# Two start-up loads of a fused attention and feed-forward kernel: issued by ScalarE instead of SyncE

## The chip, the cores and the metric

The kernel runs on one core of a Trainium2 chip. The metric is the device time of one execution in microseconds (us); lower is better. The engines are TensorE (PE; its weight loads are PEld), VectorE (DVE), ScalarE (ACT), GpSimd (POOL) and SyncE (SP). SyncE does no arithmetic: it issues data transfers (DMA), which 16 DMA engines carry out.

## The reference, cut to what matters

```python
def _attn_ref(q, k, v):                      # 8 batches, 8 heads, 576 tokens, head size 64
    scores = (1 / np.sqrt(D)) * np.matmul(q, k.transpose(0, 1, 3, 2))
    rel = pos[:, None] - pos[None, :]
    mask_local   = (rel >= 0) & (rel < 32)
    mask_strided = (rel >= 0) & (pos[None, :] % 32 == pos[:, None] % 32)
    # heads 0 to 3 use mask_local, heads 4 to 7 mask_strided
    scores = np.where(masks[None], scores, -1e9)
    ...                                      # softmax over the keys
    return np.matmul(attn, v)

def _moe_ref(x, w_in, w_out):                # 4608 tokens, 512 -> 2048 -> 512
    h = x @ w_in
    g = 0.5 * h * (1.0 + erf(h * inv_sqrt2))
    return g @ w_out
```

The attention's output, heads side by side, is the input x of the feed-forward part.

## The kernel before, in words

The 4608 tokens are worked on in nine tiles of 512. For each tile the feed-forward part runs over 16 slices of 128 hidden units. For each slice, `ffn_h` makes the hidden values H (lines L758 to L760), `ffn_g` applies the activation, and `ffn_o` adds the slice's share of the output O (L796 to L798). Each product is done three times with operands split into a high and a low part, to keep fp32 precision. The weights of a slice come as `ws` and are split on ScalarE and VectorE (`split_w`, L174 to L189). This product work keeps TensorE busy, and the attention of the later tiles is fitted in beside it on the other engines.

The first tile's attention has nothing to hide behind. It is done on TensorE, in the order that the string `START` writes out, one item after the other:

- **Local heads.** `local_job` (items L0 to L3) does four local tiles of 128 tokens. Item by item: scores S_L (L322), mask and maximum on VectorE (L280, four each), exponentials on ScalarE (L285, four each), sums and reciprocals on VectorE (L289, L292), the scaling (L298 on VectorE for tiles 2, 0 and 3, L301 on ScalarE for tile 1), transposes (L328), a copy (L330), values (L336), and the split into high and low parts (L305, L307). The order is tile 2, then 0, 1 and 3.
- **Strided heads.** `half_tile` (items a0, b0) does the two halves, called A0 and A1 here: scores (L455), mask added on VectorE with `smask` (L464), maximum (L466), difference (L468), exponential on ScalarE (L470), sum (L472), reciprocal and scaling (L474 to L478), transposes (L482) and a copy (L484). `strided_tile` (item A0 of the string) then multiplies by the values (L498), turns the result (L503) and splits it (L506, L509).
- **Fillers.** L949 multiplies zeros into a bank named busy.

The loads: q2, q0, q1 and q3 fetch queries and keys of the local tiles (`load_jq`, L222, tile `qk`, 128 rows of 2,560 B each); S0 and T0 fetch the strided queries and keys of the two halves (`load_half`, L423, tile `qka`, 128 rows of 6,144 B each, 0.786 MB); v1, v0, v2 and v3 the local values (`load_jv`, L229, tile `vl`, rows of 2,048 B); w and W items weights (`load_w`, L153), in two halves for slices 0 and 1; B0 the strided values (`load_b`, L441, tile `va`). "w0" is the weights of slice 0. Before the change all of them are issued by SyncE, in the order of the string. A transfer takes one of eight completion semaphores in turn (DMAHW0 to DMAHW7), and so the ninth waits until the first has landed, and so on.

`behind` attaches a wait from a list `hold` to a transfer; the list is filled by items p alone, which come much later. GpSimd makes the masks: `mask` (L872 to L879) for L280, `ident` (masks.py) for the transposes, `smask` (L883, L884 and L886 on VectorE), and `bmask` (L910 to L918), used first by the second tile. The order on each engine is fixed when the program is built.

Of the kernel before, what the change touches and what calls it, by code (L numbers as in the profile page):

```python
# [86 lines left out]
def attn_ffn_kernel(ctx: ExitStack, tc: tile.TileContext, qk, vl, qka, va, qs, ks, vs, s1, w, out):  # L87
    nc = tc.nc
# [42 lines left out]
    def slot(name, shape, dtype=F32):  # L131

        return wpool.tile(shape, dtype, name=name, tag="w")

    def pace(ins, after):
        if after is not None:
            tc.add_manual_dep(ins.ins, after.ins.name, mybir.DependencyInfo(
                mybir.DependencyClass.Sync, mybir.DependencyReason.DATA), reason="pace")
# [3 lines left out]
    def behind(ins):  # L142

        while hold:
            pace(ins, hold.pop())
        return ins
# [272 lines left out]
    def load_half(o):  # L419

        x = slot(f"qka_{o}", [P, 4 * DM])
        n = N2 * NGR // 2 * 32
        behind(nc.sync.dma_start(x[:, 0:3 * n], qka[0, o]))  # L423
        qa[o] = x
        kv[o] = x[:, 2 * n:3 * n].rearrange("p (a g m) -> p a g m", a=N2, m=MA)
        qv[o] = x[:, 0:2 * n].rearrange("p (n c) -> p n c", c=2 * 32)

    def load_a(t):

        nv = NGR // 4 * HL * D  # L430
        load_half(0)
        vt = slot(f"va_{t}", [P, 4 * DM])
        p = vt[:, nv:nv + NGR * 32].rearrange("p (g m) -> p g m", g=NGR)
        nc.gpsimd.memset(p, 0.0)
        ka[t] = (
                 vt[:, 0:nv].rearrange("p (c h d) -> p c h d", c=NGR // 4, h=HL),
                 p, vt[:, nv + NGR * 32:nv + 2 * NGR * 32].rearrange("p (c q) -> p c q", q=P),
                 qa[0][:, 0:NGR * D].rearrange("p (b c e m) -> p b c e m", b=4, c=NGR // 4, e=DH), vt[:, 0:nv])
# [75 lines left out]
    for vi in range(NA, NV):  # L514
        n = VISITS[vi][2]
# [465 lines left out]
    with tc.manual_schedule(engines={ET.DVE, ET.Activation, ET.PE, ET.SP, ET.Pool}):  # L981
        for it in START:
            kind = it[0]
            if kind == "p":
                hold.append(last[0])
            elif kind in "wWqvSTBEeKkVGg":
                x = int(it[1:] or 0)
                {"w": lambda x: load_w(x, 0 if f"W{x}" in START else None), "W": lambda x: load_w(x, 1),
                 "T": lambda x: load_half(1), "k": lambda x: load_keys_half(x, 1), "q": load_jq, "v": load_jv, "S": load_a, "B": load_b,
                 "E": lambda x: [load_strided(order_g[0], nm) for nm in "qk"],  # L990
                 "e": lambda x: load_strided(order_g[0], "v"),
                 "K": lambda x: load_keys(x, halves=kparts if f"k{x}" in START else None), "V": load_values,
                 "G": lambda x: [load_strided(order_g[1], nm) for nm in "qk"],
                 "g": lambda x: load_strided(order_g[1], "v")}[kind](x)
            else:
                if it not in running:
                    running[it] = job(it)
                if next(running[it], True) is None:
                    continue
                running[it] = None  # L1000
# [218 lines left out]
```

## Time and profile before

| | |
|---|---|
| median of 3 runs | 846.77 us (846.35 to 846.95) |
| profiled execution | 848.29 us |
| its span in the profile | 846.5 us |
| TensorE, busy share of the span | 99% |
| VectorE | 76% |
| ScalarE | 52% |
| GpSimd | 2% |
| mean granted clock of TensorE | 0.996 of full speed |

The span runs from the first to the last instruction of the profiled execution; 1.79 us of its time lie outside. Busy shares are means over a long kernel. The change touches the first 20 us alone, so rows of that stretch are read one by one further down.

### The profile page before, as it was taken

To read this page: it belongs to the slowest core of one execution; us is meant where nothing else is said; L and a number is where in the kernel's file an instruction comes from. 1 tells how busy PE (TensorE), PEld (TensorE's weight loads), DVE (VectorE), ACT (ScalarE), POOL (GpSimd) and SP (SyncE) were. 2 spreads that over 40 slices of the span, in tenths; PEclk is the share of its full clock that TensorE was granted. 3 is DMA by queue.
4 is the path that set the end of the run, shared out by engine and by line. 5 is a ranking of instruction groups with operands and counts; after the bars stand their busy time and mean duration, and the time that the engine had idled before them with its cause. 6 is when DMAs were issued, how large, how long until landed. Compare 5 with 4: busy or idle time off the path is not lost.

```text
span 846.5 us, 15032 instructions
## 1 busy us (share of the span) xinstructions
PE 838.3 (99%) x5442; PEld 690.0 (82%) x5442; DVE 640.3 (76%) x1859; ACT 441.0 (52%) x862; POOL 18.1 (2%) x88
## 2 busy tenths in 40 slices
PE   8999999999999999999999999999999999999997
PEld 5788888888888888888888888888888888888886
DVE  6899989995999589958999698878887988521110
ACT  6898866552664355544553266545552456332222
POOL 5000000000000000000000000000000000000000
PEclk9899999999999999999999999999999999999999
DMA  9965241211220220223021222112102310100001
GB/s 342 416 256 194 64 144 52 68 37 64 99 63 14 92 101 9 69 60 136 7 63 35 78 86 69 42 63 100 60 13 93 101 38 13 36 34 17 1 0 50
DMA packets 27978, 69.40 MB, mean 82 GB/s; under 512 B 5888, under 2 KB 14208, under 8 KB 25856
## 3 DMA queue, kind: packets, MB, share of 16 engines
q1 hardware_dynamic: 27904, 68.44, 22.9%
q8 instruction: 43, 0.70, 0.3%
q14 instruction: 31, 0.25, 0.1%
HBM read 54.78 MB, written 9.44 MB: 76 GB/s over the span
## 4 chain that ended last, share of the span: by engine, by line
PE 98%; POOL 1%; DVE 1%; issue 0%; ACT 0%; POOLq 0%
PE H L758 16%; PE H L759 15%; PE H L760 15%; PE O L796 15%; PE O L798 15%; PE O L797 15%; PE S_x L404 2%; PE S L363 1%; PE S_L L336 0%; PE busy L949 0%; PE A L498 0%; PE S_L L328 0%; POOL bmask L913 0%; PE A L455 0%; POOL bmaskNone L913 0%
## 5 line engine op out<-in xcount | busy, mean ns | idle before, releaser
L798 PE MATMUL O<-w,gl 128*128 128x512 f32 x576 | 224.1, 389 | 0.0
L797 PE MATMUL O<-w,gh 128*128 128x512 f32 x576 | 224.1, 389 | 0.0
L796 PE MATMUL O<-w,gh 128*128 128x512 f32 x576 | 224.1, 389 | 0.0
L766 ACT ACTIVATE H<-H 128x512 f32<-128x512 f32 x144 | 83.8, 582 | 259.7 <-PE H L760 252.1
L770 DVE TENSOR_TENSOR gl<-H,gh 128x512 fp32r<-128x512 f32 x144 | 99.1, 688 | 157.4 <-ACT gh L768 157.3
L768 ACT CAST gh<-H 128x512 fp32r<-128x512 f32 x144 | 84.5, 587 | 118.2 <-PE O L797 113.7
L797 PEld LDWEIGHTS O<-w,gh 128*128 128x128 f32 x576 | 108.2, 188 | 22.6
L798 PEld LDWEIGHTS O<-w,gl 128*128 128x128 f32 x576 | 108.1, 188 | 22.4
L796 PEld LDWEIGHTS O<-w,gh 128*128 128x128 f32 x576 | 108.1, 188 | 22.4
L758 PE MATMUL H<-dh,w 128*128 128x512 f32 x288 | 114.3, 397 | 0.0
L759 PE MATMUL H<-dl,w 128*128 128x512 f32 x288 | 112.3, 390 | 0.0
L760 PE MATMUL H<-dh,w 128*128 128x512 f32 x288 | 112.2, 390 | 0.0
L759 PE MATMUL H<-xl,w 128*128 128x512 f32 x288 | 112.2, 390 | 0.0
L758 PE MATMUL H<-xh,w 128*128 128x512 f32 x288 | 112.2, 389 | 0.0
L760 PE MATMUL H<-xh,w 128*128 128x512 f32 x288 | 112.1, 389 | 0.0
L653 DVE TENSOR_TENSOR av<-sv,sc 128x320 f32<-128x320 f32 (+12 forms) x192 | 102.1, 564 | 6.8 <-DMA sv<-in_vs_dram 6.5
L601 DVE TENSOR_TENSOR qk<-sk,sq 128x320 f32<-128x320 f32 (+5 forms) x200 | 103.6, 545 | 0.0
L605 DVE TENSOR_REDUCE sc<-qk 128x5 f32<-128x320 f32 (+5 forms) x200 | 102.4, 538 | 0.0
L657 DVE TENSOR_REDUCE acc<-av 128x32 f32<-128x544 f32 (+16 forms) x192 | 101.2, 556 | 0.2
L766 ACT ACT_TABLE_LOAD x51 | 65.4, 1283 | 0.9
L758 PEld LDWEIGHTS H<-dh,w 128*128 128x128 f32 x288 | 54.2, 188 | 12.2
L760 PEld LDWEIGHTS H<-dh,w 128*128 128x128 f32 x288 | 54.1, 188 | 11.5
(123 smaller groups left out, 802.8 us busy)
## 6 DMA issues: line engine op xcount, KB each, us to landing
ws<-in_w_dram SPq DMA_DIRECT2D x14, 1023.8 KB, 9.9
qk<-in_qk_dram SPq DMA_DIRECT2D x8, 1280.0 KB, 5.6
vl<-in_vl_dram SPq DMA_DIRECT2D x8, 1024.0 KB, 4.8
out_dram<-ob SPq DMA_DIRECT2D x32, 256.0 KB, 2.3
sk<-in_ks_dram SPq DMA_DIRECT2D x8, 576.0 KB, 4.9
sv<-in_vs_dram SPq DMA_DIRECT2D x8, 576.0 KB, 3.8
band<-PT_L SPq DMA_DIRECT2D x224, 16.0 KB, 1.8
sq<-in_qs_dram SPq DMA_DIRECT2D x4, 448.0 KB, 3.6
```

Source lines behind the costliest of these rows:

```text
L601: nc.vector.tensor_tensor(tmp, sq[vi, "k"][:, c0:c1, :], sq[vi, "q"][:, r0 + r, :].unsqueeze(1).to_broadcast([P, n, D]), ALU.mult)
L605: nc.vector.tensor_reduce(ss[u][:, r, c0:c1], at[0], AX.X, ALU.add)
L653: nc.vector.tensor_tensor(tmp, sq[vi, "v"][:, d0:d1, 0:wr], ss[u][:, r, 0:wr].unsqueeze(1).to_broadcast([P, n, wr]), ALU.mult)
L657: nc.vector.tensor_reduce(ss[u, "acc"][:, r, d0:d1], at[0], AX.X, ALU.add)
L758: last[0] = nc.tensor.matmul(hp, w1[f][:, 0, c, :], xh, start=(i == 0), stop=False)
L759: last[0] = nc.tensor.matmul(hp, w1[f][:, 0, c, :], xl, start=False, stop=False)
L760: last[0] = nc.tensor.matmul(hp, w1[f][:, 1, c, :], xh, start=False, stop=(i == NC - 1))
L766: gelu[n] = nc.scalar.activation(hp, hp, AF.Gelu)
L770: nc.vector.tensor_tensor(gl, hp, gh.bitcast(F32), ALU.subtract)
L796: last[0] = nc.tensor.matmul(o, gh[:, sl], w2[f][:, 0, :], start=(f == 0), stop=False)
L797: last[0] = nc.tensor.matmul(o, gh[:, sl], w2[f][:, 1, :], start=False, stop=False)
L798: last[0] = nc.tensor.matmul(o, gl[:, sl], w2[f][:, 0, :], start=False, stop=(f == NF - 1))
```

## The change

```diff
@@ load_half @@
         x = slot(f"qka_{o}", [P, 4 * DM])
         n = N2 * NGR // 2 * 32
-        behind(nc.sync.dma_start(x[:, 0:3 * n], qka[0, o]))
+        nc.scalar.dma_start(x[:, 0:3 * n], qka[0, o])
         qa[o] = x
```

`load_half` runs twice, for S0 and T0. At both places `hold` is empty, so leaving `behind` out takes no wait away. The transfers now stand in ScalarE's order and use ScalarE's queue. The orders of TensorE and VectorE are the same as before; those of ScalarE, SyncE and GpSimd differ.

On ScalarE, at the start of the program (`early` holds tile 2's scores, `pbig` those of tile 0; a + is a row of the change alone):

```order
 L1215 UNCONDITIONAL_BRANCH
+L423 DMA qka_242<-in_qka_dram 128x1536
 L889 ACT_TABLE_LOAD
 L889 ACTIVATE warm<-warm 128x1
 L285 ACTIVATE early,ss_L_213<-early,nm_L_212 128x96 x4
+L423 DMA qka_254<-in_qka_dram 128x1536
 L285 ACTIVATE pbig,ss_L_227<-pbig,nm_L_226 128x96 x4
```

The first half's transfer (qka_242) became ScalarE's first instruction; the second half's (qka_254) stands behind the four exponentials of local tile 2.

On SyncE, before, with the semaphores that an issue waits for (qk are the local queries and keys, vl the local values, ws_312 the weights of slice 0, ws_375 those of slice 1):

```order
L222 DMA qk_91<-in_qk_dram 128x640 x3
L423 DMA qka_242<-in_qka_dram 128x1536
L423 DMA qka_254<-in_qka_dram 128x1536
L222 DMA qk_91<-in_qk_dram 128x640
L229 DMA vl_276<-in_vl_dram 128x512 x2
L229 DMA vl_276<-in_vl_dram 128x512 [waits DMAHW0_49]
L153 DMA ws_312<-in_w_dram 128x2048 [waits DMAHW1_49]
L441 DMA va_244<-in_va_dram 128x1024 [waits DMAHW2_49]
L153 DMA ws_375<-in_w_dram 128x2048 [waits DMAHW3_49]
L153 DMA ws_312<-in_w_dram 128x2047 [waits DMAHW4_49]
L229 DMA vl_276<-in_vl_dram 128x512 [waits DMAHW5_49]
```

and in the change:

```order
L222 DMA qk_91<-in_qk_dram 128x640 x4
L229 DMA vl_276<-in_vl_dram 128x512 x2
L229 DMA vl_276<-in_vl_dram 128x512 [waits DMAHW0_49]
L153 DMA ws_312<-in_w_dram 128x2048 [waits DMAHW1_49]
L441 DMA va_244<-in_va_dram 128x1024 [waits DMAHW2_49]
L153 DMA ws_375<-in_w_dram 128x2048 [waits DMAHW3_49]
L153 DMA ws_312<-in_w_dram 128x2047 [waits DMAHW4_49]
L229 DMA vl_276<-in_vl_dram 128x512 [waits DMAHW5_49]
```

The two transfers are gone from SyncE. The semaphores went to other transfers, though. Before, numbers 0 to 5 were those of q2, q0, q1, the first and the second strided half, and q3. Now they are those of the first strided half, q2, q0, q1, q3 and the second strided half. So the fourth value transfer, which waited for q3 (DMAHW5), now waits for the second strided half.

On GpSimd, before, around the making of `ident` and `smask` (bmaskNone is one of the masks for the second tile, va the strided probabilities' zero fill):

```order
L878 COPY pbig<-pbig 128x64
L879 MEMSET pbig 128x32
masks.py:197 MEMSET ident 128x128
L434 MEMSET va_244 128x512
L910 MEMSET bmaskNone 128x64
masks.py:199 AFFINE_SELECT ident<-ident 128x128
L883 IOTA smask 32x32 x4
L913 AFFINE_SELECT bmaskNone<-bmaskNone 32x64
L915 AFFINE_SELECT bmaskNone<-bmaskNone 32x64
```

and in the change, the same place and what leads up to it:

```order
L876 AFFINE_SELECT pbig<-pbig 64x96
L915 AFFINE_SELECT bmaskNone<-bmaskNone 32x64
L913 AFFINE_SELECT bmaskNone<-bmaskNone 32x64
L878 COPY pbig<-pbig 128x64
L879 MEMSET pbig 128x32
masks.py:197 MEMSET ident 128x128
L915 AFFINE_SELECT bmaskNone<-bmaskNone 32x64
L913 AFFINE_SELECT bmaskNone<-bmaskNone 32x64
masks.py:199 AFFINE_SELECT ident<-ident 128x128
L883 IOTA smask 32x32 x4
L915 AFFINE_SELECT bmaskNone<-bmaskNone 32x64
```

Seven of the eight L913 and L915 of bmaskNone, which all followed `smask`, now stand ahead of it (four of them are seen here, three further up); the fills of va and bmaskNone moved ahead of `mask`.

## Rows read from the trace of the kernel before

**Rows 1.** The page: busy time, share and instructions of TensorE, and the chain that ended last, its share by engine.

```profile
PE 838.3 (99%) x5442; PEld 690.0 (82%) x5442; DVE 640.3 (76%) x1859; ACT 441.0 (52%) x862; POOL 18.1 (2%) x88
...
PE 98%; POOL 1%; DVE 1%; issue 0%; ACT 0%; POOLq 0%
```

**Rows 2.** Busy time by stretch: the stretch in us, its length, busy us (and instructions) of PE, PEld, DVE, ACT and POOL, the granted clock, the DMA engines' busy share, GB/s.

```profile
0.00:20.40 20.40, 16.64 (x396) 11.96 (x397) 12.23 (x65) 13.45 (x48) 11.92 (x54) 0.99 0.91 340
20.40:27.00 6.60, 6.60 (x59) 4.39 (x57) 4.89 (x12) 4.13 (x10) 0.00 (x0) 0.50 1.00 413
27.00:841.70 814.70, 814.70 (x4991) 673.66 (x4990) 623.14 (x1783) 422.84 (x804) 6.20 (x34) 1.00 0.21 73
```

**Rows 3.** Timeline of TensorE: start and duration in us, engine, line, operation, out<-in, shapes, records (a product in fp32 has two), and in brackets the idle time before it and what ended it. The second row holds the scores of tiles 0 and 1, the fourth those of A0 and A1.

```profile
3.70 1.54 PE L322 MATMUL S_L<-qk 64*64 64x96 f32 x16
...
6.33 1.62 PE L322 MATMUL S_L<-qk 64*64 64x96 f32 x32
9.24 0.61 PE L328 MATMUL S_L<-ident,early 128*96 128x128 f32 x4 [1.29 <-POOL bmask L913]
9.78 2.06 PE L455 MATMUL A<-qka 128*64 128x32 f32 x64
...
18.21 0.34 PE L498 MATMUL A<-va 32*32 32x64 f32 x17 [0.48 <-DVE va L484]
19.68 0.79 PE L498 MATMUL A<-va 32*32 32x64 f32 x47 [1.13 <-issue]
...
26.39 0.78 PE L758 MATMUL H<-dh,w 128*128 128x512 f32 x1
```

**Rows 4.** Timeline of SyncE's issues: start and duration in us, the queue, line, what is loaded, count.

```profile
0.73 1.35 SPq L222 DMA_DIRECT2D qk<-in_qk_dram  x3
2.13 0.91 SPq L423 DMA_DIRECT2D qka<-in_qka_dram  x2
3.08 1.43 SPq L222 DMA_DIRECT2D qk<-in_qk_dram  x1
...
11.25 0.33 SPq L229 DMA_DIRECT2D vl<-in_vl_dram  x1
```

**Rows 5.** The same issues, each in a stretch of its own (those that start at 0.73, 2.13, 2.6 and 11.25 us): what is loaded, queue, operation, count, KB, and us from issue to landing.

```profile
qk<-in_qk_dram SPq DMA_DIRECT2D x1, 320.0 KB, 2.9
...
qka<-in_qka_dram SPq DMA_DIRECT2D x1, 768.0 KB, 6.4
...
qka<-in_qka_dram SPq DMA_DIRECT2D x1, 768.0 KB, 7.8
...
vl<-in_vl_dram SPq DMA_DIRECT2D x1, 256.0 KB, 8.8
```

**Rows 6.** Busy time by stretch, columns as in rows 2; the last column, GB/s, times the stretch gives the bytes moved in it.

```profile
1.00:2.00 1.00, 1.00 (x86) 0.97 (x70) 0.00 (x0) 1.00 (x1) 0.81 (x4) 1.00 0.33 41
2.00:3.00 1.00, 1.00 (x2) 0.11 (x1) 0.00 (x0) 0.21 (x2) 0.94 (x5) 1.00 0.75 243
3.00:4.00 1.00, 0.98 (x5) 0.30 (x6) 0.00 (x0) 0.00 (x0) 0.90 (x6) 1.00 1.02 393
4.00:5.00 1.00, 1.00 (x16) 0.95 (x12) 0.36 (x2) 0.00 (x0) 0.77 (x4) 1.00 0.94 338
5.00:6.00 1.00, 1.00 (x6) 0.50 (x2) 0.70 (x7) 0.40 (x3) 0.77 (x4) 1.00 0.77 265
0.00:9.00 9.00, 7.16 (x148) 4.51 (x148) 2.81 (x22) 4.39 (x18) 6.97 (x36) 1.00 0.75 268
0.00:13.00 13.00, 10.92 (x233) 7.83 (x234) 6.44 (x41) 7.19 (x29) 10.10 (x48) 1.00 0.83 299
```

**Rows 7.** DMA in the first 60 us: packets, MB and share of the one data queue. The issues of that stretch are 30 loads of 128 rows each and eight copies (L395) of 32 rows of 512 B.

```profile
q1 hardware_dynamic: 4704, 21.10, 88.2%
```

**Rows 8.** Timeline of VectorE, columns as in rows 3. The second row is L280 of tile 2, the third that of tile 0; the L464 shown is that of A1, the L484 also.

```profile
4.23 0.18 DVE L884 TENSOR_SCALAR smask<-smask 128x32 uint32<-128x32 uint32 x1 [3.37 <-POOL smask L883]
...
5.30 0.26 DVE L280 CUSTOM_DVE_ANT_0 early<-S_L,pbig 128x96 f32<-128x96 f32 x1 [0.68 <-PE S_L L322]
...
7.34 0.26 DVE L280 CUSTOM_DVE_ANT_0 pbig<-S_L,pbig 128x96 f32<-128x96 f32 x1 [1.24 <-PE S_L L322]
...
8.05 0.17 DVE L289 TENSOR_SCALAR ss_L<-ss_L 128x4 f32<-128x4 f32 x1
...
8.47 0.62 DVE L298 TENSOR_TENSOR early<-early,rs_L 128x384 f32<-128x384 f32 x1
...
12.21 0.42 DVE L464 TENSOR_TENSOR va<-A,smask 128x256 f32<-128x256 f32 x1
...
17.73 0.42 DVE L484 COPY va<-A 128x256 f32<-128x256 f32 x1 [0.53 <-PE A L498]
```

**Rows 9.** Timeline of ScalarE, columns as in rows 3: the first and the last instruction of tile 2's exponentials, and the first of tile 0's.

```profile
5.60 0.37 ACT L285 ACTIVATE early<-early,nm_L 128x96 f32<-128x96 f32 x1 [3.38 <-DVE nm_L L280]
...
6.96 0.19 ACT L285 ACTIVATION_READ_ACCUMULATOR early<-early,nm_L 128x1 f32 x1
7.64 0.37 ACT L285 ACTIVATE pbig<-pbig,nm_L 128x96 f32<-128x96 f32 x1 [0.50 <-DVE nm_L L280]
```

**Rows 10.** Timeline of GpSimd, columns as in rows 3: the first and the sixth of eight instructions in a row on bmaskNone.

```profile
4.26 0.24 POOL L913 TENSOR_SCALAR_AFFINE_SELECT bmaskNone<-bmaskNone 32x64 f32<-32x64 f32 x1
...
5.72 0.23 POOL L915 TENSOR_SCALAR_AFFINE_SELECT bmaskNone<-bmaskNone 32x64 f32<-32x64 f32 x1
```

## The prediction

> **What bounds the kernel now.** I began with the chain that ended last: TensorE holds 98% of it, and it is busy for 99% of the span [rows 1]. A change at the very start can then matter only by moving the moment from which TensorE never stops. The busy times by stretch give that moment: from 20.4 to 27.0 us it is busy for 6.60 of 6.60 us at a granted clock of 0.50 (1.2 GHz), and from 27.0 to 841.7 us for all of 814.70 us at 1.00 (2.4 GHz) [rows 2]. Nothing after 20.4 us holds a gap in which a late start could be caught up, so each microsecond by which the first L758 product (26.39 us, [rows 3]) slips is a microsecond of the span, as long as the clock behaves as before. All idle time of TensorE that can be filled lies before 20.4 us: 20.40 less 16.64, 3.8 us.
>
> I then followed TensorE, VectorE and ScalarE backwards from 26.39 us. TensorE runs without a gap from 19.68 us, after a stop of 1.13 us that the trace puts down to "issue" [rows 3]. Before that stop it had waited 0.48 us for VectorE's L484 copy, which began at 17.73 us [rows 3, 8]. That copy ends the softmax of the second strided half (A1), whose first step on VectorE is the second L464, at 12.21 us [rows 8]. From 12.21 to 17.73 us the two strided halves and the local tile 3 share VectorE in a fixed order, with no wait of note. So two things set the start: when A0's scores (L455) can run, and when A1's can. The 64 records of L455 take 2.06 us from 9.78 us [rows 3], 32 for each half; A1's therefore start at about 10.8 and end at 11.84 us, 0.37 us before VectorE takes them. A1 may slip 0.3 us free of charge, no more: A1's scores may begin at 11.1 us.
>
> A0's scores stand behind the transposes of local tile 2 (9.24 us), those behind L298 on VectorE (8.47 to 9.09), L298 behind L289 (8.05), and L289 in order behind the four L280 of local tile 0 (7.34), which wait for TensorE's L322 of tile 0 (6.33) [rows 3, 8]. That one stands behind a filler, and all behind tile 2's scores at 3.70 us, which waited for the first transfer, q2 [rows 3]. So the landing of q2 at 0.73 + 2.9 = 3.63 us [rows 4, 5] sets A0, and A0 starts 9.78 - 3.63 = 6.15 us after it.
>
> **Step 1: the first moved transfer.** SyncE issued it at 2.13 us behind three key transfers [rows 4]. ScalarE now issues it as its first instruction, so at about 0.73 us, beside q2. It is not needed before 9.78 us, so its earlier arrival (it landed at 2.13 + 6.4 = 8.5 us [rows 4, 5]) gains nothing. What it can do is take bandwidth from q2. In the trace of before all data goes through one queue, so two queues at once are not shown and I bound it. q2 has 0.328 MB, the new neighbour 0.786 MB. From the per-microsecond rates the bytes moved are 0.04 by 2, 0.28 by 3, 0.68 by 4 and 1.02 MB by 5 us [rows 6]; q2's 0.328 MB were through at 3.1 us and it counted as landed 0.5 us later. No contention: 3.63 us. Equal bytes: 0.656 MB are through at 3.95 us, landing 4.45. Equal packets: the 30 plain loads of the first 60 us have 128 rows each, with 256 packets of 512 B and 16 small ones for each of the 38 transfers that is 3840 + 256 + 608 = 4704, the count in the row [rows 7]; so a packet is a row, both transfers have 128, and q2 is through only with its neighbour, 1.114 MB, at 5.4 us, landing 5.9. I take 5.4 us, near the packet end, because whole rows are what the queue moves. A0 is then 1.8 us late: its scores run from 11.55 to 12.6 us.
>
> The Trainium skill, "DMA: Bandwidth & Descriptors", section "Queues, rings and completion order", says that each DMA engine takes turns between the queues it has work for, a whole packet at a time. By that rule alone q2 would land at 5.9 us and A0 be 2.3 us late; no row here shows two data queues competing.
>
> **Step 2: GpSimd's order.** Seven instructions of bmaskNone (0.29 us apart: six steps take 5.72 - 4.26 us for five intervals [rows 10]) now stand ahead of the smask iota. VectorE's L884, which waited for it until 4.23 us [rows 8], comes at 4.23 + 2.0 = 6.25, and L280 of tile 2 no earlier than 6.65 us instead of 5.30. With q2 at 5.4, L280 waits for TensorE until 5.4 + 1.67 = 7.07 us anyway, so the masks cost nothing. Without contention that cover is gone: ScalarE's four L285 would end at 8.5 instead of 7.15 us, L289 would wait for them from 8.05, and A0 would be 0.5 us late.
>
> **Step 3: the second moved transfer.** It stands on ScalarE behind the four L285 of tile 2. These began at 5.60, 0.30 us after L280, and ended at 6.96 + 0.19 = 7.15, so 1.85 us after L280's start [rows 8, 9]. Now 7.07 + 1.85 = 8.9 us, against an issue at about 2.6 us before (the second of a pair that takes 0.91 us [rows 4]). With the masks alone it is 8.5 us. From issue to landing: q2 needed 2.9 us, of which 0.83 is its bytes at 393 GB/s [rows 5, 6], so at most 2.07 fixed; some of that is the slow first microsecond, so at least 1.2 (hardly a byte moves before 2 us, 1.27 us after the issue [rows 6]). Its 0.786 MB take 2.0 us alone at 393 GB/s. SyncE's queue is full then, though: by 9 us 2.4 MB have moved [rows 6] of 5.0 MB (four keys, the first moved transfer, three values, two halves of w0, one of w1 and the strided values: 1.31 + 0.79 + 0.79 + 2.10). In turns of packets with rows of 2048 to 4096 B it takes 2.6 to 3.3 us, in equal bytes 4.0. The bounds of the landing are 8.5 + 1.2 + 2.0 = 11.7 and 8.9 + 2.1 + 4.0 = 15.0 us; I take 8.9 + 1.5 + 3.0 = 13.4 us. Before it was 2.6 + 7.8 = 10.4 [rows 5].
>
> TensorE takes its work in order, so A1's 32 L455 stand still until 13.4 us, and with them the scores of local tile 3, the filler and everything up to L498. Measured against 11.1 us that is **2.3 us**. It contains step 1's 1.8 us; the two don't add, since A0's part of the softmax is done while A1 is waited for.
>
> **Step 4: what costs nothing.** Each issue takes ScalarE 0.45 us (half of 0.91 [rows 4]). The first lies in its wait until 5.60 us, 3.38 us long; the second in the wait before the L285 of tile 0, which would start at 7.64 + 1.8 = 9.4 us and is free at 9.35 [rows 9]. SyncE saves 0.91 us and issues the fourth keys at 2.1 instead of 3.08 us; these are used after A1, so this isn't on the path. SyncE's fourth value transfer waits for the second moved transfer now (its semaphore, in the order of SyncE), so it goes out at 13.4 instead of 11.25 us; with the 8.8 us it took before it lands at 22.2, and L336 of tile 3 stands right ahead of the first L758, so a little before 26.39 + 2.3 us [rows 3 to 5]. The queue does not run dry: by 13 us 3.9 of 5.8 MB have moved [rows 6].
>
> **The sum.** 2.3 us on the span of 846.5 gives 848.8. The profiled execution took 848.29 us, 1.79 more than its span, so the changed kernel's would take 850.6. The median of the three runs, 846.77, is 1.5 us below the profiled one, and the shift is the same there: **849.1 us**, +0.27%. About 0.2% (1.7 us) is what a measurement of this kernel can tell from no change.
>
> **The rivals.** *Nearly hidden.* The two queues hardly disturb each other and the second transfer lands at 11.7 to 12.3 us: shift 0.6 to 1.2 us; or the stop of 1.13 us at 18.55 us, whose cause isn't shown, falls into the new wait, 2.3 - 1.1 = 1.2. About 847.8 us. For it: SyncE's rates do sag to 265 GB/s between 5 and 6 us [rows 6], so there is room. Against it: the second issue cannot leave before 8.5 us.
>
> The Trainium skill, same page, section "Issuing engines are not separate DMA queues", has it that another issuing engine saves only the issue time. The 0.91 us saved on SyncE are off the path, so by that sentence alone the time would stay at 846.8 us; it leaves out the place of the instruction in ScalarE's order, which is what I price.
>
> *Larger.* An issue into a busy system takes longer: SyncE's fourth took 1.43 us [rows 4]. With 1 us more on ScalarE and equal bytes the landing is 16.0 us, the shift 4.9, the time 851.6. Nothing of before shows ScalarE issuing.
>
> *Faster.* The half-clock stretch of 6.6 us [rows 2] follows the wait and the stop around 18 to 19.7 us. If the later start puts TensorE's work closer together there, the clock stays at 2.4 GHz: at most 3.3 us back, about half of it before VectorE's low parts become the bound, and the stop's 1.1 us. That is 2.7 us; it decides only if the shift stays under it by 1.7, so with the second transfer at its earliest: 0.6 - 2.7, about 844.7 us. Against it: the new waits, at 4 to 5 and at 12.6 to 13.4 us, are more idle time, not less.
>
> **How the numbers follow.** The forecast has 0.50, its own range 848.2 to 850.6 (landing of 12.5 to 14.9 us); nearly hidden 0.27; larger 0.17; faster 0.06. Slower by over 0.2% (above 848.5) is 0.46 of the first and the 0.17: 0.63. Within 0.2%: 0.04 and 0.27, 0.31. Faster: 0.06. The range 846.9 to 851.4 leaves out the faster case, a little of the hidden one and half of the larger: 0.2.
>
> **What would show it.** Tile 2's L322 near 5.4 us, not 3.7; L280 of tile 2 at 6.65 us or later; ScalarE's second issue at 8.5 to 9 us; a wait of TensorE in front of the second half of L455 until about 13.4 us; the first L758 near 28.7 us; from there a span that ends 2.3 us later. I would be wrong if q2 landed at 3.6 us, if A1's scores ran by 11.5 us, or if the half-clock stretch changed its length by more than a microsecond.

## The result, and the profile after

The changed kernel takes 853.36 us (median of 4 runs, 853.01 to 853.63), the kernel before 846.59 (4 runs, 846.35 to 846.95). The ratio is 1.0076, 95% interval 1.0061 to 1.0091: slower by 0.76%, or 6.8 us. The forecast was 849.1 us, its range ended at 851.4. The direction and the places were right, the size was not. The profiled execution took 853.35 us; its span is 851.6.

TensorE in the profile after, rows as in [rows 3]:

```profile
5.85 1.54 PE L322 MATMUL S_L<-qk 64*64 64x96 f32 x16 [2.17 <-DMA qk<-in_qk_dram]
...
12.35 1.13 PE L455 MATMUL A<-qka 128*64 128x32 f32 x32
16.66 1.93 PE L455 MATMUL A<-qka 128*64 128x32 f32 x32 [3.18 <-DMA qka<-in_qka_dram]
18.52 1.55 PE L322 MATMUL S_L<-qk 64*64 64x96 f32 x16
19.99 2.08 PE L949 MATMUL busy<-const-float32-0.0 128*128 128x512 f32 x2
21.86 1.06 PE L328 MATMUL S_L<-ident,pbig 128*96 128x128 f32 x4
22.85 0.85 PE L336 MATMUL S_L<-PT_L,vl 96*64 96x64 f32 x16
...
31.86 0.50 PE L758 MATMUL H<-dh,w 128*128 128x512 f32 x1
```

L455, one row of 64 records before, is two rows now: A0's 32 records at 12.35 us, then a wait of 3.18 us, and A1's 32 at 16.66. What follows A1 runs at half rate up to 22.85 us. The first L758 comes at 31.86 us.

The issues of the two moved transfers on ScalarE, with what stands between them (timeline of ScalarE, ACTq is its queue):

```profile
0.73 0.41 ACTq L423 DMA_DIRECT2D qka<-in_qka_dram  x1
...
7.75 0.37 ACT L285 ACTIVATE early<-early,nm_L 128x96 f32<-128x96 f32 x1 [5.08 <-DVE nm_L L280]
...
8.29 0.34 ACTq L423 DMA_DIRECT2D qka<-in_qka_dram  x1
```

Their landings, from the DMA view of the moments at which they were issued (us from issue to landing is the last number; compare [rows 5]):

```profile
qka<-in_qka_dram ACTq DMA_DIRECT2D x1, 768.0 KB, 5.3
...
qka<-in_qka_dram ACTq DMA_DIRECT2D x1, 768.0 KB, 8.3
```

So the first half is there at 6.0 us and the second at 8.29 + 8.3 = 16.6. The chain of work that ended last now goes through two loads, q2's and the second half's, where the chain of the profile before held none (its rows in order of time: start, length, what):

```profile
0.73 5.07 DMA qk<-in_qk_dram
...
8.29 8.33 DMA qka<-in_qka_dram
16.66 1.93 PE A L455 x32
```

Busy time by stretch, columns as in [rows 2]:

```profile
0.00:16.60 16.60, 9.26 (x184) 6.35 (x184) 5.95 (x37) 7.00 (x28) 11.40 (x54) 0.99 0.90 332
16.60:23.30 6.70, 6.64 (x63) 4.81 (x64) 4.15 (x22) 3.46 (x14) 0.00 (x0) 0.50 0.79 300
23.30:31.80 8.50, 7.28 (x210) 5.57 (x206) 6.22 (x15) 6.35 (x14) 0.00 (x0) 1.00 1.00 404
31.80:847.00 815.20, 815.20 (x4998) 673.50 (x4992) 624.16 (x1786) 423.61 (x806) 6.19 (x34) 1.00 0.20 71
```

From 16.6 to 23.3 us the granted clock is 0.50 (1.2 GHz), right behind the wait for the second half. From 31.8 us on TensorE is never idle again.

### The profile page after: what moved, and what is told of

Read it like the earlier page. It is cut to its first block, busy times and chain, and to the rows that moved or that the text cites. A ratio compares the mean times of both kernels' runs of the same rounds, so it can differ in the third digit from the quotient of the medians.

```text
span 851.6 us, 15033 instructions
## 1 busy us (share of the span) xinstructions
PE 838.5 (98%) x5442; PEld 690.2 (81%) x5442; DVE 640.5 (75%) x1859; ACT 441.0 (52%) x862; POOL 17.6 (2%) x88
## 3 DMA queue, kind: packets, MB, share of 16 engines
q10 hardware_dynamic: 288, 1.57, 0.5%
## 4 chain that ended last, share of the span: by engine, by line
PE 97%; DMA 2%; ACT 0%; DVE 0%; issue 0%
PE H L758 16%; PE H L760 15%; PE O L797 15%; PE H L759 15%; PE O L796 15%; PE O L798 15%; PE S_x L404 2%; PE S L363 1%; DMA qka<-in_qka_dram 1%; DMA qk<-in_qk_dram 1%; PE S_L L322 0%; PE busy L949 0%; ACT dh L506 0%; PE A L455 0%; PE S_L L336 0%; PE S_L L328 0%
## 5 line engine op out<-in xcount | busy, mean ns | idle before, releaser
L797 PE MATMUL O<-w,gh 128*128 128x512 f32 x576 | 224.2, 389 | 0.0
L796 PE MATMUL O<-w,gh 128*128 128x512 f32 x576 | 224.1, 389 | 0.0
L798 PE MATMUL O<-w,gl 128*128 128x512 f32 x576 | 224.0, 389 | 0.0
L797 PEld LDWEIGHTS O<-w,gh 128*128 128x128 f32 x576 | 108.1, 188 | 22.8 <-DVE w L189 0.4
L796 PEld LDWEIGHTS O<-w,gh 128*128 128x128 f32 x576 | 108.1, 188 | 22.5
L798 PEld LDWEIGHTS O<-w,gl 128*128 128x128 f32 x576 | 108.1, 188 | 22.4
L758 PE MATMUL H<-dh,w 128*128 128x512 f32 x288 | 114.0, 396 | 0.0
L760 PE MATMUL H<-dh,w 128*128 128x512 f32 x288 | 112.2, 390 | 0.0
L758 PE MATMUL H<-xh,w 128*128 128x512 f32 x288 | 112.2, 389 | 0.0
L760 PE MATMUL H<-xh,w 128*128 128x512 f32 x288 | 112.1, 389 | 0.0
L759 PE MATMUL H<-dl,w 128*128 128x512 f32 x288 | 112.1, 389 | 0.0
L759 PE MATMUL H<-xl,w 128*128 128x512 f32 x288 | 112.0, 389 | 0.0
L758 PEld LDWEIGHTS H<-dh,w 128*128 128x128 f32 x288 | 54.0, 187 | 12.1
L760 PEld LDWEIGHTS H<-xh,w 128*128 128x128 f32 x288 | 54.1, 188 | 11.4
```

Of the source, the lines that this page charges most:

```text
L758: last[0] = nc.tensor.matmul(hp, w1[f][:, 0, c, :], xh, start=(i == 0), stop=False)
L759: last[0] = nc.tensor.matmul(hp, w1[f][:, 0, c, :], xl, start=False, stop=False)
L760: last[0] = nc.tensor.matmul(hp, w1[f][:, 1, c, :], xh, start=False, stop=(i == NC - 1))
L796: last[0] = nc.tensor.matmul(o, gh[:, sl], w2[f][:, 0, :], start=(f == 0), stop=False)
L797: last[0] = nc.tensor.matmul(o, gh[:, sl], w2[f][:, 1, :], start=False, stop=False)
L798: last[0] = nc.tensor.matmul(o, gl[:, sl], w2[f][:, 0, :], start=False, stop=(f == NF - 1))
```

## The experiments

The theory: the kernel loses what A1's scores are late, and again what TensorE then loses at half clock. The lateness comes from the place of the second transfer behind what SyncE issued ahead of it. The rivals: ScalarE's queue as such does it; the first transfer's competition with q2 does it; the clock has nothing to do with it.

### The kernel before once more

> The kernel before, unchanged, for a second profile: the profiled execution of before took 848.3 us and its unprofiled runs 846.4 to 846.9, while for the changed kernel the two agree. Theory: the stop of 1.13 us put down to issue, or the half-clock stretch of 6.6 us, differs between executions of before, and a second profile near 846.6 us will lack the one or have it shorter. Rival: the profile itself costs before 1.7 us; then the second looks like the first, at about 848.3.

847.44 us (11 runs, 846.56 to 849.72), ratio 1.0002. The profiled execution took 846.56 us with a span of 844.8, where the one shown ahead of the prediction had 848.29 and 846.5. TensorE:

```profile
3.93 1.54 PE L322 MATMUL S_L<-qk 64*64 64x96 f32 x16 [0.25 <-DMA qk<-in_qk_dram]
...
10.53 2.06 PE L455 MATMUL A<-qka 128*64 128x32 f32 x64
...
14.82 0.69 PE L336 MATMUL S_L<-PT_L,vl 96*64 96x64 f32 x16
...
23.86 0.50 PE L758 MATMUL H<-dh,w 128*128 128x512 f32 x1
...
32.38 0.50 PE L797 MATMUL O<-w,gh 128*128 128x512 f32 x1 [0.88 <-DVE w L185]
```

No stop for "issue" and no half-clock stretch here; the first L758 comes 2.5 us earlier than in [rows 3], and a wait of 0.88 us stands ahead of L797 instead. Executions of this kernel differ by such things (845.9 to 850.3 us over all that were timed), and the one that the prediction was read from was 1.7 us longer than this one. In what follows the changed kernels are compared with this profile.

### One half at a time

first_only moves the first half alone, second_only the second:

```diff
-        behind(nc.sync.dma_start(x[:, 0:3 * n], qka[0, o]))
+        behind((nc.sync if o else nc.scalar).dma_start(x[:, 0:3 * n], qka[0, o]))   # first_only
+        behind((nc.scalar if o else nc.sync).dma_start(x[:, 0:3 * n], qka[0, o]))   # second_only
```

> Only the first strided half is issued by ScalarE; the second is back on SyncE, behind q2, q0 and q1. GpSimd keeps the order of the change. Theory: two separate losses make up the change, and this run holds the first alone: the transfer beside q2 delays q2 to about 5.8 us (5.85 us in the changed kernel, 3.70 before), and everything up to the first hidden product slips with it by 2.2 us, because the second half has landed by about 10 us and nobody waits for it. Time about 848.8 us. Rival 1 (q2's delay is hidden and the second half alone costs the 6.8 us): within 0.5 us of before, 846.6. Rival 2 (GpSimd's order of masks sets the start): L280 of tile 2 would begin right behind the smask, at 6.6 us, with TensorE's scores done well before.

848.22 us (11 runs, 847.34 to 850.9) against 847.28: ratio 1.0009 (0.9999 to 1.002). TensorE:

```profile
6.13 1.55 PE L322 MATMUL S_L<-qk 64*64 64x96 f32 x16 [2.45 <-DMA qk<-in_qk_dram]
...
12.71 2.06 PE L455 MATMUL A<-qka 128*64 128x32 f32 x64
...
26.06 0.50 PE L758 MATMUL H<-dh,w 128*128 128x512 f32 x1
...
33.88 0.50 PE L797 MATMUL O<-w,gh 128*128 128x512 f32 x1 [0.15 <-issue]
```

q2 is late by 2.2 us, and so are A0 and A1, which run without a gap, and the first L758. The wait ahead of L797 shrinks from 0.88 to 0.15 us, so that 1.5 us are left at L797 and in the span (846.3 against 844.8).

> Only the second strided half is issued by ScalarE, behind the first of tile 2's exponentials; the first half is on SyncE as before, and GpSimd's order is that of before. Theory: q2 lands at 3.6 us as before, ScalarE issues at about 6.1 us, the transfer's first bytes come only after what SyncE has issued by then (some 3 us later, as in the changed kernel), and it lands at 13.3 to 14.4 us instead of 10.4. A1's scores start there instead of 10.8, a loss of 2.2 to 3.3 us, and one to two more if the wait of TensorE brings its clock to 1.2 GHz: 849 to 851.5 us. Rival (the landing is late only because q2 and the exponentials are late in the changed kernel): 847 us or less.

851.66 us (5 runs, 851.39 to 852.31), ratio 1.0052 (1.0039 to 1.0066). q2 is not disturbed (L322 at 3.75 us); the second half, issued at 6.19, lands 8.4 us later:

```profile
10.08 1.12 PE L455 MATMUL A<-qka 128*64 128x32 f32 x32
14.58 1.93 PE L455 MATMUL A<-qka 128*64 128x32 f32 x32 [3.38 <-DMA qka<-in_qka_dram]
```

The wait and the half clock behind it are those of the changed kernel. From 14.5 to 21.5 us the granted clock is 0.54. So the second transfer carries most of the loss; the first one's delay of q2 comes on top, because the second issue stands behind tile 2's exponentials.

### Is it ScalarE's queue, or what is ahead of the transfer?

quiet is the changed kernel, but SyncE holds its value and weight loads back after the four key loads until tile 1's scores are made (an item p0, which fills `hold`), so that the second half finds the DMA engines free:

```diff
-q3 L2 L1 v1 L2
+q3 L2 L1 p0 v1 L2
```

> The changed kernel with SyncE held after its four key transfers until local tile 1's scores are done (about 10.5 us), so that SyncE has nothing new under way when ScalarE issues the second half at 8.3 us; all later loads come some 7 us late, so the time as a whole says nothing and will be several us longer. Theory (in the changed kernel the second half's first bytes waited 3.1 us because SyncE's earlier issues stood ahead of it, whatever queue they were in): its bytes start by 9.5 us and it lands at about 12 us, not 16.6. Rival (ScalarE's issue takes 3 us to start in itself while the engine works): first bytes at 11.4 us, landing near 14.

850.16 us (one run, span 848.4). Issued at 8.20 us, the second half lands 4.2 us later:

```profile
qka<-in_qka_dram ACTq DMA_DIRECT2D x1, 768.0 KB, 4.2
```

L455 is one row of 64 records at 12.38 us, at full clock, and the first L758 comes at 26.72. What is left of the loss are q2's delay and the held loads, which are late in their turn (TensorE waits 1.03 us for va at 20.48 us, and 1.50 ahead of L797).

sync_late leaves ScalarE out. It is the kernel before with the second half issued by SyncE late, behind half of w0 and the strided values:

```diff
-q1 S0 L0 L2 T0 L1 L2 L2 q3
+q1 S0 L0 L2 L1 L2 L2 q3
-a0 a0 b0 L3 a0 b0 L1 b0 a0 b0 B0 L1
+a0 a0 B0 T0 b0 L3 a0 b0 L1 b0 a0 b0 L1
```

> ScalarE issues nothing here: the kernel of before, except that SyncE issues the second strided half late, behind the first half of slice 0's weights and the strided values (and these strided values a little earlier in the order of the string). The second half has 4.46 MB ahead of it in the one queue and 0.79 MB of its own; at 350 GB/s from 2 us on that is a landing of 16 to 17 us, as late as in the changed kernel, while local tile 2's scores stay at 3.9 us. My theory: only the landing counts, so A1's scores wait until 16 to 17 us, TensorE falls to half clock behind the wait for about 6 us, and the time is 852 to 853.5 us. Rival: the loss belongs to the second queue (its competition with SyncE's, or the clock's reaction to it); then A1's scores run at full clock and the first L758 comes only 4 us later than before, the time 849.5 to 850.5.

853.91 us (4 runs, 852.86 to 854.55), ratio 1.0074 (1.0057 to 1.0091): the loss of the changed kernel, without its change. (In SyncE's order 3.93 MB stand ahead of the second half, not 4.46 as expected.) A1's scores start about as late, at 16.94 us; the wait is longer, 5.89 us, since A0 is done earlier. The granted clock from 16.9 to 23.0 us is 0.50. TensorE:

```profile
9.92 1.12 PE L455 MATMUL A<-qka 128*64 128x32 f32 x32
16.94 1.92 PE L455 MATMUL A<-qka 128*64 128x32 f32 x32 [5.89 <-DMA qka<-in_qka_dram]
```

sync_late shows that the loss follows the late landing, whichever queue carries the second half. quiet shows that ScalarE's queue lands the same bytes 4.2 us after the issue where little else is in flight, against 8.3 us in the changed kernel. For the changed kernel the DMA view shows this by stretches. The rows are those of 4 to 5, 10 to 11, 11.7 to 11.8 and 13 to 14 us, and the last that of quiet from 9.1 to 9.2 us; q10 is ScalarE's queue, q1 SyncE's; packets, MB, share of the 16 engines:

```profile
q10 hardware_dynamic: 51, 0.31, 75.7%
q1 hardware_dynamic: 47, 0.12, 28.8%
...
q1 hardware_dynamic: 130, 0.40, 114.6%
...
q1 hardware_dynamic: 11, 0.04, 90.6%
q10 hardware_dynamic: 1, 0.01, 14.6%
...
q10 hardware_dynamic: 41, 0.25, 61.5%
q1 hardware_dynamic: 41, 0.16, 39.8%
...
q10 hardware_dynamic: 3, 0.02, 202.1%
```

Where both queues have packets in flight they take turns, 51 to 47 and 41 to 41. But after the issue at 8.29 us q10 moves nothing until the stretch that starts at 11.7 us, 3.4 us later, while q1 keeps the engines full; in quiet, issued at 8.20 us, it was 0.9 us. SyncE had issued 3.15 MB by 8.29 us; q1 had moved 1.46 MB of them by then and 2.68 MB by 11.7 us. So most of that backlog went first, though not all of it, and from its first packet on the second queue shared. Whether the bytes ahead alone hold the first packet back, or a second queue also starts late in itself when the engines are full, no run separates.

### Both transfers at once, and the first one cut in two

both_early puts T0 next to S0, so that ScalarE issues both at the start (0.73 and 1.24 us):

```diff
-q1 S0 L0 L2 T0 L1
+q1 S0 T0 L0 L2 L1
```

> Both halves are issued by ScalarE, the second right behind the first and the table load, at about 2.7 us, ahead of all exponentials. Theory (the place behind the exponentials costs most): TensorE no longer waits for the second half, its clock stays at 2.4 GHz, and what is left is the contention at the start: q2 at 5.8 us, q0 and q1 a little later than in the changed kernel, 8.5 to 9 us. Loss 2.2 to 2.8 us against before, 849 to 849.5 us, 4 us faster than the changed kernel. Rival (any transfer through ScalarE's queue starts 3 us after its issue once SyncE has a backlog, and lands after 8 us): the second half lands near 11 us, which is still before A0 is done at 13.5, so the same time, but later bytes in the second queue: from about 6 us rather than 3.

854.4 us (4 runs, 853.08 to 854.72), ratio 1.008 (1.0066 to 1.0093). This missed by 5 us. The second half lands at 10.2 us and A1 waits for nothing, but the three key transfers of SyncE now share the engines with 1.57 MB:

```profile
1.61 2.08 PE L898 MATMUL lead_in<-const-float32-0.0 128*128 128x512 f32 x2
...
9.91 2.82 PE L322 MATMUL S_L<-qk 64*64 64x96 f32 x32 [1.29 <-DMA qk<-in_qk_dram]
14.59 3.63 PE L455 MATMUL A<-qka 128*64 128x32 f32 x64
...
28.01 1.13 PE L949 MATMUL busy<-const-float32-0.0 128*128 128x512 f32 x2
...
30.47 0.50 PE L758 MATMUL H<-dh,w 128*128 128x512 f32 x1
```

q0 lands at 9.9 us, and tiles 0 and 1 are 3.4 us later than in before_again (6.56). I had priced q2 alone and forgotten that q0 has the same neighbour. But that is only half of the 6.6 us by which the first L758 is later than in before_again. From tile 0's scores to the L328 at 21.10 us TensorE takes 11.2 us, where before_again takes 7.7 (6.56 to 14.29): L455 takes 3.63 us instead of 2.06, half rate.

The row of 10.0 to 20.5 us reads a granted clock of 1.00 all the same. The reason is that this trace's first record of the clock begins at 20.69 us, and a row counts time without a record as 1.00. The durations show what the row doesn't: the lead-in's two records of 512 columns at 1.61 us take 2.08 us, two of the same form at 28.01 us take 1.13. All the traces here begin with that half rate (2.07 or 2.08 us for the lead-in), and it ends where the first record begins: at 6.53 us in the execution of [rows 6], 7.99 in before_again, 20.69 here.

halves is first_only with the first half as two transfers of half the row length:

```diff
-        behind(nc.sync.dma_start(x[:, 0:3 * n], qka[0, o]))
+        if o:
+            behind(nc.sync.dma_start(x[:, 0:3 * n], qka[0, o]))
+        else:
+            for i in range(2):
+                cs = slice(i * 3 * n // 2, (i + 1) * 3 * n // 2)
+                nc.scalar.dma_start(x[:, cs], qka[0, o, :, cs])
```

> As first_only, but ScalarE issues the first half as two transfers of 128 rows of 3,072 B instead of one of 6,144 B. Theory (the two queues take turns row by row): beside q2's 128 rows of 2,560 B only the first of the two is moved, so q2 is through after 0.72 MB instead of 1.11 and lands at about 5.1 us instead of 6.1; the first hidden product comes 1 us earlier than in first_only, near 25 us. Rival (a second queue delays the start of the first one's data, or takes its share whatever the rows): q2 lands at 5.9 us or later, as in first_only.

847.76 us (12 runs, 847.35 to 852.0), ratio 1.0006 (0.9992 to 1.0019): no difference to first_only that can be measured. The mechanism held: with rows of 3,072 B beside q2's 2,560 B, L322 of tile 2 starts at 5.25 us instead of 6.13. Most of the gain is lost one tile later, since q0 now shares as well (tile 0 at 8.59 us, 8.76 in first_only). What follows in this profile is no guide to a usual execution: it was taken in one of the two longest of the twelve (851.35 us), in which the half rate of the start lasts until 19.89 us and the first product of the hidden values comes at 29.28.

### The clock

fill is the changed kernel with three fillers of 512 columns between A0's and A1's scores; second_fill is second_only with the same three:

```diff
-a0 a0 b0 L3
+a0 a0 z0 z0 z0 b0 L3
```

> The changed kernel with three more fillers of 512 columns ahead of A1's scores, which fill the 3.2 us in which TensorE waits for the second half (13.5 to 16.7 us). Theory: of the 6.8 us that the change costs some 3 are the clock: from A1's scores to the end of the next filler the same instructions took 1.93 + 1.55 + 2.08 + 1.06 us in the changed kernel and 1.03 + 0.88 + 1.13 + 0.60 in the second profile of before. With the fillers the clock stays at 2.4 GHz, A1 starts at 16.7 to 17 us as before, and the first hidden product comes near 29 us instead of 31.9: about 850.4 us. Rival (VectorE and ScalarE set the pace of that stretch, the half clock is hidden behind them): the first hidden product stays within 1 us of 31.9 and the time above 852.4 us.

> The second half alone on ScalarE (the first on SyncE, as in second_only), with the same three fillers ahead of A1's scores. Theory: lateness and clock add up in second_only's loss, about 2.8 us and 3 us at the first hidden product (29.65 us there, 23.86 in the second profile of before); with the fillers it comes near 26.8 us, and the time falls from 851.7 to about 849.0 us. Rival: as for the fillers on the changed kernel, no more than 1 us gained.

fill took 852.83 us (5 runs, 852.71 to 854.71; ratio 1.0071, 1.0058 to 1.0085), second_fill 850.58 (6 runs, 850.27 to 853.83; ratio 1.0045, 1.003 to 1.0061): 0.5 and 1.1 us less than without fillers, where 3 and 2.7 were expected. Against the kernel before as timed beside each, the losses are 5.8 us instead of 6.8 and 3.5 instead of 4.4; the intervals overlap. In fill's profile A1's scores come at 16.97 us and take 1.13 us instead of 1.93, and the first L758 comes at 29.17 instead of 31.86: 2.7 us were gained there. They were lost again in a stop of 2.38 us, put down to "issue", ahead of an L759 at 37.81 us, and in 3.4 us at half clock behind it. second_fill's profile has a stop of 1.83 us ahead of the same L759; it cannot test its theory, since the half rate of the start lasts until 17.04 us there, the fillers take 5.39 us instead of 3.50, and A1's scores come at 18.12. Both profiles happened to be of their kernel's longest execution, so a typical one was wanted.

### The stop that took the gain back

> The kernel fill once more, for another profile: its first one was taken in its slowest execution and showed a stop of 2.38 us at 37.8 us. If such stops are chance, this profile has none, a span of 850.9 us or less, and its first L758 near 29.2 us; what is lost after it must then be seen in stalls before L797 or a stretch at half clock. If the stop belongs to the kernel, it is there again.

852.73 us, span 850.9; the first L758 at 29.41 us, and the stop is there again, ahead of the same instruction:

```profile
29.41 0.50 PE L758 MATMUL H<-dh,w 128*128 128x512 f32 x1
...
35.30 0.39 PE L758 MATMUL H<-xh,w 128*128 128x512 f32 x1
37.24 0.40 PE L759 MATMUL H<-xl,w 128*128 128x512 f32 x1 [1.55 <-issue]
```

A gain of 2.45 us at L758 less 1.55 is 0.9; the spans differ by 0.7. fill_four and fill_two have four and two fillers:

```diff
-a0 a0 z0 z0 z0 b0 L3
+a0 a0 z0 z0 z0 z0 b0 L3      # fill_four
+a0 a0 z0 z0 b0 L3            # fill_two
```

> fill with four fillers ahead of A1's scores instead of three. All three profiles of kernels with three fillers stop 1.6 to 2.4 us ahead of the same instruction, the second L759 on xl of the first slice's third row block, at 37.2 to 38.4 us, for nothing that the profile shows. Theory: TensorE has reached an instruction that isn't there yet (its code), so the stop is tied to a count of instructions from the program's start: one filler more (one or two products in that count) moves it one or two products earlier, to L758 on xh or the L760 ahead of it. Rival: the stop waits for data or for something that the profile doesn't show there, and stays ahead of the L759 on xl. The fourth filler takes 1.1 us at full clock, A1's scores start at about 17.5 us, the first L758 at 29.5.

855.57 us (one run), span 853.8:

```profile
35.80 0.40 PE L759 MATMUL H<-dl,w 128*128 128x512 f32 x1
38.22 0.59 PE L760 MATMUL H<-dh,w 128*128 128x512 f32 x1 [2.02 <-issue]
```

> fill with two fillers instead of three. By the theory of the code the stop comes one or two products later than the L759 on xl, ahead of L760 or the L758 behind it; by the rival it stays ahead of the L759 on xl. If TensorE falls to half clock again, since it waits about 1.2 us longer for A1's scores, it gets there later and the stop is short or gone, which tells nothing apart.

851.26 us (one run), span 849.5:

```profile
16.48 1.12 PE L455 MATMUL A<-qka 128*64 128x32 f32 x32 [0.67 <-DMA qka<-in_qka_dram]
...
28.68 0.50 PE L758 MATMUL H<-dh,w 128*128 128x512 f32 x1
...
35.01 0.40 PE L760 MATMUL H<-xh,w 128*128 128x512 f32 x1
36.35 0.39 PE L758 MATMUL H<-xh,w 128*128 128x512 f32 x1 [0.95 <-issue]
```

A slice's products go L758, L759, L760 on dh and dl, twice, then the same on xh and xl, twice, then L796 to L798. The stop stands ahead of the 6th product of this slice with four fillers, the 8th with three, the 10th with two: each filler is two products, and moves it by exactly two. It is tied to a count of instructions from the start of the program, not to data. Without fillers that count is the 14th product, the L797 that waited in first_only and before_again. The records of TensorE in the traces, weight loads and its few waits and jumps included, say the same without exception: exactly 1,217 of them stand ahead of the stop in each of the ten profiles that have it (also quiet, both_early, halves and second_fill), and 705, 512 fewer, ahead of the stop in [rows 3].

The DMA view has a partner for it: one packet of an instruction queue (q8), here in fill_two from 33.9 to 34.0 us.

```profile
q8 instruction: 1, 0.02, 67.1%
```

TensorE goes on 2.45 us after the start of that stretch. The same pair is 2.54 us apart in fill_again (34.7 and 37.24), 2.52 in fill_four (35.7 and 38.22), 2.38 in first_only (31.5 and 33.88), 2.48 in before_again (29.9 and 32.38) and 2.68 for the stop in [rows 3] (17.0 and 19.68); the packet is the second of its queue in the span there, and the fourth in the others. Each run's page has 43 packets of q8 for some 11,050 records of TensorE, 257 to a packet, so the 512 records between the two stops are two packets' worth. In the changed kernel the packet moves at 36.7 and the L797 of the count is reached at 39.33, 2.63 us later, without a stop. So I read these stops as TensorE waiting for the next piece of its own program: the count of instructions and the packet both say so. The profile's releaser in before_again, VectorE's L185, had ended 0.66 us before TensorE went on. What starts that packet, and why it is not fetched earlier, no row shows. The Trainium skill, "Runtime: NRT & Kernel Launch", section "Terms", says that an engine's instruction memory is refilled in blocks of 16 KiB. The packet's 0.02 MB agree with that; that TensorE can wait for such a block is what the pairs and the count add. That full DMA engines are the reason is not shown.

## Why the prediction was wrong

**What bounds the kernel: right, but for one gap.** All that was lost at the start was lost in the span, up to the first L797. From there on the changed kernel and before_again need the same time to the end of the span: 851.6 - 39.33 = 812.3 and 844.8 - 32.38 = 812.4 us. The forecast saw no gap behind 20.4 us in which a late start could be caught up; before_again has one, the 0.88 us ahead of L797.

**Step 1, q2: right.** It was put near the equal-packet end, at 5.4 us of 3.63 to 5.9; L322 started at 5.85, A0 at 12.35 us against 10.53, so 1.8 us late, as forecast. The Trainium skill, "DMA: Bandwidth & Descriptors", section "Queues, rings and completion order", says that turns are taken a packet at a time; the trace agrees, with 51 packets against 47 in one microsecond, though the one queue moved 0.31 MB and the other 0.12. What the step left out is that q0 and q1 share too, which both_early and halves showed.

**Step 2, GpSimd's order: right.** L884 came at 6.17 us (6.25 said) and L280 of tile 2 at 7.45, released by TensorE:

```profile
6.17 0.18 DVE L884 TENSOR_SCALAR smask<-smask 128x32 uint32<-128x32 uint32 x1 [5.30 <-POOL smask L883]
...
7.45 0.26 DVE L280 CUSTOM_DVE_ANT_0 early<-S_L,pbig 128x96 f32<-128x96 f32 x1 [0.88 <-PE S_L L322]
```

**Step 3, the second transfer: the term that was mis-sized.** The issue came at 8.29 us, 0.6 us before the forecast, since it does not wait for the exponentials ahead of it to finish. The landing came at 16.6 us instead of 13.4, 8.3 us after the issue where I allowed 4.5. "1.5 fixed plus 3.0 for the bytes" let the transfer share almost from its issue on. Its first packet moved only 3.4 us after the issue, its last large one 4.1 us later (in the stretch from 15.7 to 15.8 us), and it counted as landed 0.8 us after that: 4.2 us beside the bytes where I allowed 1.5, and 4.1 us for the bytes where I allowed 3.0. The issue rows of the page before and the bytes by 9 us [rows 4, 6] had shown how full the queue was; I used that for the rate and not for the start. The rival "larger" gave 16.0 us and so nearly the landing, for another reason: its dearer issue did not come (0.34 us).

**The clock: the step that failed.** It was taken as neutral, with a stretch that might even vanish. The kernel before has no such stretch in its usual execution, and the changed one has 6.2 us of it, right behind the wait that the change makes. The runs say the same: 6.8 us at half clock lower an execution's mean granted clock to 0.996, which all four executions of the changed kernel have (0.995 or 0.996), while 17 of the 21 executions of the kernel before that were timed beside first_only have 0.998 or more. From A1's scores to the L336 at 22.85 us it takes 6.19 us; in before_again the same work takes 3.26 (from 11.56, which is 10.53 and half of 2.06, to the L336 at 14.82). That is 2.9 us, which neither "larger" nor the range had in it. fill_two, in its one execution, confirms the price: two fillers in the wait, A1 at 16.48 us, hardly earlier, full clock, and the first L758 at 28.68 instead of 31.86.

**Step 4, what costs nothing: right for what it named.** ScalarE's issues hid, and v3, which went out at 16.64 us behind the second half, is waited for by nobody.

**The sum, redone from the rows.** A1's scores are 16.66 - 11.56 = 5.1 us later than in before_again, and the half clock adds 2.9: 8.0, which is how much later the first L758 is (31.86 - 23.86). TensorE's wait for its program at L797, 0.88 us in before_again, is gone, and from L758 to that L797 the changed kernel takes 7.47 us instead of 8.52: 1.05 back. 6.95 are left; the spans differ by 6.8 and the medians by 6.8. The forecast's 2.3 us lacked 2.8 of lateness and the 2.9 of the clock, and did not know of the 1.1 given back.

**The base: "the shift is the same there" failed with it.** The execution that I read was 1.7 us longer than that of before_again, by a wait for code and a half-clock stretch that are not part of every execution. "The stop whose cause isn't shown" was that wait for code. The sum took the shift from this profile and added it to the median unchanged. It is not the same: between the two profiles the span grew by 5.1 us (846.5 to 851.6), between the medians by 6.8. The half-clock stretch is about as long in both profiles (20.4 to 27.0 us there, 16.6 to 23.3 here), so against the execution that I read the clock cost nothing new, and the sign "if the half-clock stretch changed its length" stayed silent; against a usual execution it cost the 2.9 us.

**The rival of the issuing engine.** The Trainium skill, same page, section "Issuing engines are not separate DMA queues", has another issuing engine save only issue time. By that alone the time would have stayed. It was 6.8 us longer. sync_late, which loses as much without ScalarE's queue, puts the loss on the late landing: on the place in time that the second transfer was given with the queue.

No kernel tried beats the kernel before. The best, halves and first_only, cannot be told from it.

## What to carry to other kernels

A transfer moved to another engine's queue takes its place among the bytes in flight at the time of its new issue: price the start of its first byte behind the backlog, then the sharing, and do the same for each transfer that it will share with. A new wait of TensorE can have a second price, the half clock on what follows, here 2.9 us behind a wait of 3.2; read it from a stretch of the same trace that shows it, and add it to the sum. Read two executions of the kernel before you take a stall of 1 us for a property of it, or carry a shift from one profile over to a median.

## What the runs showed of the hardware that I had not expected

- A second queue hardly overtakes: its first packet moved 3.4 us after the issue with the engines full, 0.9 us when SyncE held its loads back.
- Late in the start-up TensorE seems to outrun its own program. It goes on 2.4 to 2.7 us after an instruction packet has moved, in waits of 0.15 to 2.4 us. The profile calls the wait "issue", or names the last semaphore, as it did with L185; so microseconds gained ahead of that point are partly taken back (1.55 of 2.45 in fill_again), and microseconds lost are partly given back (1.05 of 8.0).
- TensorE starts every execution profiled here at half rate, and the clock rows read 1.00 until the trace's first record of the clock. The half rate ended at 6.5 to 20.7 us; in both_early it made L455 take 3.63 us instead of 2.06. Why it lasted so long there, no run tells.
